# Windowed attention on one core: which tiles of the array make the values of VectorE and ScalarE, and where the two halves of a score pair run

## The chip, the cores and the metric

The kernel runs on one core of one Trainium2 chip. The metric is the device time of one execution in microseconds (us); lower is better. The engines of the core work side by side and wait for one another through semaphores: TensorE (PE in the profile; its weight loads are PEld), VectorE (DVE), ScalarE (ACT), GpSimd (POOL) and SyncE (SP), which here only issues DMAs.

## The reference, cut to what matters

An image of 224 x 224 tokens with 96 channels is projected to q, k and v. The first 48 channels attend within horizontal stripes of 8 rows, the last 48 within vertical stripes of 8 columns. Each stripe has 8 x 224 = 1792 tokens; there are 28 horizontal and 28 vertical ones. The two results are put side by side and projected with `wo`.

```
qkv = einsum('bhwc,cd->bhwd', x, wqkv)
qh, kh, vh = first 48 channels of q, k, v, as 28 stripes of 8 rows   (28, 1792, 48)
oh = softmax(qh @ kh^T * 48**-0.5) @ vh
qv, kv, vv = last 48 channels, as 28 stripes of 8 columns            (28, 1792, 48)
ov = softmax(qv @ kv^T * 48**-0.5) @ vv
out = concat(oh, ov) @ wo
```

## The kernel before, in words

**Stages.** Two stripes are worked on at a time, one in partitions 0 to 63 and one in 64 to 127 (`w` in the code). So there are 28 stages `P`: 0 to 13 for the horizontal stripes, 14 to 27 for the vertical ones. In each stage the 1792 queries are cut into four chunks `c` (512, 512, 512, 256), and the 1792 keys into 28 key tiles of 64.

**Units.** The work on scores comes in units: two key tiles by 512 queries (four key tiles by 256 in the last chunk). A unit's scores (`qk`, L764) fill two PSUM banks, the two *halves* of a pair; each half is written by two matmuls, one per stripe, for each key tile. A unit belongs to ScalarE or to VectorE (L437 to L446):

- A ScalarE unit (`add_a`, L820): scores (stream `a`), one exponential over both banks (`A`, L824) into a tile `PT`, then one value product (`c`).
- A VectorE unit (`add_d`, L832): scores (stream `b`), VectorE turns each half into integers `I_sb` (`j`, L844), and two further tiles `U_sb` and `E_sb` are made from it (L849, stream `U`) by GpSimd, or by VectorE where the order string has a small `u`. Each of the three tiles goes into a value product of its own (`d`, `d`, `D`), so that a VectorE unit has three value products where a ScalarE unit has one.

There are 984 ScalarE units and 388 VectorE units; `ND` = "4442" gives the VectorE units per chunk, so that a stage has 35 ScalarE units and 14 of VectorE (stage 0: 39 and 10).

**Tiles of the array.** With 48 or 49 rows of contraction and 64 or fewer output columns, TensorE is used as four tiles of 64 x 64. A matmul from partitions 64w to PSUM partitions 64w is on a *diagonal* tile (mode `q` in the code), one from 64w to 64 - 64w on an *off-diagonal* tile (mode `v`). The two stripes of one mode go side by side, and the two modes can go side by side too. In general scores are on the diagonal tiles and value products off them; for *turned* key tiles (`turned`, L463: the first 2 x TURN, TURN = 2) it is the other way round. `TD` = "1111" says how many of a chunk's VectorE units are among the turned ones. So before, in each of the first three chunks, units 0 (VectorE) and 1 (ScalarE) are turned, units 2 to 4 are VectorE's and 5 to 13 ScalarE's, not turned.

**Preparation.** While stage P is worked on, `prep` (L506) makes K, Q and V of stage P+1: projections on TensorE, evacuated into `KT_sb`, `QT_sb`, `V_sb` (two buffers each). For it, `blocks` (L403) copies two stripes of x into a DRAM buffer `x_blocks` (two DMAs), and `load` (L413) reads that back transposed (two DMAs) once the copies have landed. In the vertical half, `fin` (L671) writes the stage's output at its end with 24 stores (L760), when the last addition on GpSimd (L733) is done.

**The order of the work** is written out by hand in two strings. In `SEQ` each letter takes the next operation of one stream, so that the order of the letters fixes the order on every engine; `BANK` gives the PSUM bank of each new tile. The letters of SyncE's queue are `x` (start), `X` (block copies and loads) and `y` (stores). Engines take their operations strictly in this order (`emit`, L250): an operation that waits holds up all that is behind it on its engine. Semaphore waits are derived from the operations' dependencies (`place`, L200).

Of the kernel before, what the change touches and what calls it, by code (L numbers as in the profile page):

```python
# [6 lines left out]
BF16 = mybir.dt.bfloat16  # L7
# [9 lines left out]
TURN = 2  # L17
TD = ["1111"]
# [5 lines left out]
def ndc(P, c):  # L24
# [9 lines left out]
    "fDjDAbcaceadfdAjdadaddecUdbAdadjafcDcAXXDebacajcbcUAcajcacbccAjcfaadodffAdbkeUadaddgjADbDacarjcbcAacrackcUjbdA"
    "fcacaejdfdAdabeadfdfUAXjcfabacecdAXcdadjabDdDAjbcacaDjfDAcaceUacDccAbaoaDcjbAgadardUjfdfAdfadradDfeADacaeccbVc"
    "fAajcaccbecAacjacUdbdAajdadbdjbddADaDajDdUDAacDcacbcDcAjdbacacjdUbAcajdadbdAodaDaDdjcdAcUdadagcbcArDcracacDcjA"
    "bcUacajgccAraodardbdgAdajUdadfDrAgarDacecfAcacreacUcbAdardadfdjdAbDaDeaDfDAdjacacdecdUAbdadjaDbDcAXXajcacbccAj"
    "bkcaUcacjcccAfadoadfdfAadaedkdbUcgAjcbDaDajcfcAacraecrbcfUcAjdadadebdAadadjdbdcdAXcjaUbaDdjDDAXabaffjDfAcDeacU"
    "accDAbcacjacccbcAoadaUdfjdAagadedffdfAracracDfDAebaUacecfcAcaedajdbdAadjbdadVdcjdAcbDaDjaDbDAdcUjacacbcdAcjaca"
    "cbcDAcjacUabDoAadadjdgddAdcrabraUcdDjdADbaDajDcbcAacjacfcUcAcaecagccAoadrardggUADaraDrddfrAdbrdacacjbcAUacacef"  # L40
    "cDAjDaDaDbecfAcaceacDdjbkdAadkajdDbdAjaUabdddddAXXjcacacbcAcjbacaUcccjcAfadaodfDfAbDaedadUgdjAdbacacrjcbcAaDra"
    "DDfjUDbAadadejdfdAadeaddcdcAXUbacajbdcdAXcDjabaDcjAcbUacacjcfcfAacaccfcbAoaaUcegAdadrajdfdAdraDaDfefdfAUabaecf"
    "ccjAbcacaecfcAcaVjcacbdedAadjbdadjbdAdUDaDajDdDbAcacjacbcdAcjaUcabdcDjbADcadajdAbdaodaUcdcdjcAdadagcbDrADDraca"
    "UcDcjbAcacajccgcAoaadrdbrUdgAdadrajDfDAdragacecfUAcacreaccfdAraddadbedfAdacajcbDADeaDajbkdDdkAcjdaUdaDbDcAXXaj"
    "cacbccAjbcacaUcjcccAfadoadfdfAadaedbdUDfAjDbcacaejcbcAacajcgdbUdArdajdadfrdAaDeaDdbdDAXUDjdabaccjdcAXfafafcbec"
    "DAacUacjcbcDAcajbacccjcAbadUaodfDAdjadadfdfefAaDageUcbcAracraccfjcAacacebcVcfAjadaddbedAadjbdaUDdDjdADbDacjacb"
    "cAdcjacaUcdbDAcajcabDoAdadadjUgdAdDarDarcdcbAcdajbadcDUcAjgaaccrDcrbAacacjccAUaodadbggAjdadadrdbArDaDarcjfUcAc"
    "acradfdedAadacebcfdAdjacacdDeAUbdaDajDbdADdjaDabcDjAXXcbcUacajcfcAcaecacbccAjafakcUofAdfdaaeddbAgdajdaDbDkrcAr"
    "aUcadjfdbdAcaecjadfcAcaceaUcfdfAXfadeabdDDdAXjafaDdbedADacaUjcDcbAcacjacbcDAcjabacccjcUAbaadodfDffAjadaddfedAa"
    "ceacVDbcfAjcacacbecAacUjadbddjbdAagadjdddDAaDrUaDrDbcdAjcaacbccdAcjabaUcDjcDAbacajdbddAjadacUcbocdAdaadjDgDdAc"  # L50
    "argarcDUcDArcarcacbcAccjcadaodbUAaDjaDcfcdgAbedadacrcjbAUdadadrfddAjgaadeddcAdcUarcarbdcAdDjabaDDjAfDaDaeUfcDc"
    "AXXaceacbccAjbacaccjkcccAfkadoaUdffAdaedadgdbArDfarDaccUejbAcacacjbcfdAdjadadbedAacacjbfdfAXcfjabUacDedDAXdadj"
    "abDdDAjDcacUacbcAcDjacaccccAbaoadUdfdjAdfadaedfDfAaDeagcfUcrAbracacedfAdadaeddjbAcVacajcbccAjbacaccjbDUAddaacj"
    "dcDbADaDjacbcdAcjdUcabaoDADajbadgddAjadUaDdrDdrcAbadajdcbcADcjacUagDcArcbrcacaccjAcaadoUdfdAadeadDgbDArdajcacf"
    "UcrAcbdaedadfdAjdadagebDADaDrajbDAcracUacdjcdAbdadjabcDcAXXDjcacaUcbcAacjacfcccecAfaodadbkdfUAgdjadadfrbDAraDa"
    "ceccAakjacUbddfjdbAdacaecjfdAdaceaUcdDdAXbaDajbdDdDAXDjabaDcUjcbAcacajccffAcfcaeacccUAcboaaddfjDAagaDedffAdfUr"
    "dardacfcAeabacecfdAcaVjcacbceAadjbdaddjbAddacacjUdDDAaDbaDcjbcdAacjacbcdcUAjabacDcjDbAadaodcAcjbUadadgjcdADdad"
    "rabrDdcADcjaUgacDrcAbrcacaccjcAaoadUdbdfAjdadadeDgbADacracjUbccAracagjcfdAdardeadfUdAcracaddecdAbacajDdbdDAjaf"
    "aDeDDDAXXbcaucaccAjbcakcakcjcccAfaodaUdfdfADbaeDaddgjAdbDaDarjUDbDAacracfcjcbAcacaejcfcAbadeaUdDdDAXdjabadddjd"
    "cAXdadabucfAcfacjacfcAbecacacjccAcbaoadUdfcAjaDaDbedfAfadjadfUdbAecaaccfjcAcbeacagcjVAdadadbrdfrdAadaDeUdDjdDA"  # L60
    "bcacjaDcbAcdjacacbUccdAjabaccDjDbAadaodDUAdjbadaDdcjdAcgadarbcrdcADUcacjacbcADcjagaccrcAoaUdardbdgAjdadadbrcfA"
    "rDDajcaUgcAaecacfcrDrAbcacadefdAdajdabdedAdUDaDajDdbAdadjabcDcDAXXjcaUcacbcfAcjacacccecAfaodakdbUDfADfjadadebd"
    "AdgaacrcrckcAUajadfdddbeAacajcbdfdAjcacaDdeDUdAXbdDajbaDDcAXDjabadcjcbUAcacjacffAcfcaeacccAbcUoadadfjdAbadaedf"
    "fAdfjaDgaDecbAUacrjaddbdAracacfcjcAacacVefdcbAecadajdbcdUAcjdcacaDbDAaDjbDacdcjdAbUacajcDbDAaodaddjbgAdaUDarDj"
    "dcdAcdardabcDcAjDgacUacrcbrAacacjccbAcoadajUdbAgdajgaddrdAbrDaDarcjfUcAcacracfcAedadadfedAdUadeabdcdcAjdbaDaDj"
    "dDAafabcecAXXjDDDakcakcbucAacacjbcccccAjafUadodfdfAadaedgdbDArDarcaUcfjcbAcacaejcbdfAdjdadadefUdfAabaDdjDdDAXD"
    "faceabcdAXcDUjabaDcdjcbAacjaccfcAacUeaccccbAoadadfjDfAfabeadgdjAbVdadarDjbcAcacracfUcjAcbcacaeDfDAadeadjdbdUAa"
    "dajddcdcdAcacaDbDDcAjbUcacacjDcAdcabaoddAaDajDUgcDcrDAdrabaddcjbcAdadjaUbcdcAjgaaccrcbrAacacoUcAjadadbDfAjDada"
    "dedgUAbdacracjbccAracagjcfdADarDeaUDfDAdradadDedDAbadajcdUbdcAdjabadcjcAXXfcacaecbcAkcjbackacccjcAUfaadodffAad"
    "eaddgbdArDfarDacUcejbcAacacjbcfDAdjabadedUAadadjbfdfAXfjacacdcedcAXabadjcbcdAaDjaDDfcAuacaccDebDUAcacajbccAoad"  # L70
    "adfjfgAfadeaddfdrAVacracDbeDfAcacaedUdjAabdadjbddddAcjacacbcdDuAaDaDdjDbcAUacjacbccDAjacabcDjbAdaUdajdbdAcajca"
    "cbDAodDadadUjcdgcAacragrDcDcAacracrbcUcAjcccadaodbAdajdadgdfDrADragaUdebdAcacrajdbdAcracacfjcAbadeadUdDdDAjdba"
    "DaDjdcAfaafceDUcDAXXcaceacbcAacjacbccjkcccAafkadodfUdfAadaedgdbDArDarcacfjcbUAcadeajdbdfAdjdadacedcAbcacjabdDd"
    "AXDjabUaDdDjfAXcfafabecDAcDacjUaccbcAajcaccccbAoaaddUfjgAdadaedffdfAracracfDDeAbaUcaecfcAceacajcbdAadjbdadVdjb"
    "AddaDajDdDbDAacuaccdjcbAUcdacjaccbAcDajbacDjAbaUdadoddddAjacacgDDAfrarUaDcDcdAegacacdrcrbAcacajcccAbodajadcbAa"
    "cjbdUaddfjcAadaDeDgbcAcarjgaUcdrAdbadrjaddfdAracacDUdeDdAbaDajbdDdAcDjaDabcUAXXcfjcacaecbcAacjaccccfAkobUdaadj"
    "dffAadeaddbDgAjDackaUcbrcfArcacaecjbdfAccjacacfebfAUaDaDjbfDAXedadadfjdAXdddaeabDdAcdjUacaccbcDAjacaccccbAoaaU"
# [191 lines left out]
def bass_standalone__window_attn_cswin__vision_kernel(  # L269
# [32 lines left out]
    with es:  # L302
# [203 lines left out]
        def prep(P, startup=False):  # L506
# [154 lines left out]
            for f, *args in work:  # L661
                f(*args)
# [272 lines left out]
```

## Time and profile before

| | |
|---|---|
| median of 3 runs | 947.76 us (947.38 to 948.65) |
| the profiled execution's own time | 947.77 us |
| its span, first to last instruction | 945.7 us |
| busy: PE, ACT, DVE, POOL | 99%, 98%, 93%, 81% of the span |
| exponentials on ScalarE (L824) | 984 |
| stores of the vertical half (L760) | 312 in 13 stages |
| block copies (L411), transposing loads (L418) | 54, 54 |
| mean granted TensorE clock | 0.997 |

How to read it: the profile is one execution. Engines' busy shares say which engine could be the limit; matmuls are pipelined, so a busy PE is not PE at its peak. A group of the profile is a line of the code with an engine, an operation and tiles; its numbers are busy time, the mean duration of one, and the idle time of the engine before it with what ended that. Issues of DMAs stand under SPq. The "granted clock" is the share of its full clock that TensorE got.

### The profile page before, as it was taken

Reading aid. Unit: us, or ns where it says so; the run is one execution under the profiler, and the core shown is the slowest. Engines: PE = TensorE matmul, PEld = TensorE weight load, DVE = VectorE, ACT = ScalarE, POOL = GpSimd, SP = SyncE. Lnnn points to the kernel's source line nnn. Section 1 sums busy time; section 2 is a strip of 40 time slices with the busy share of each in tenths; the row PEclk is TensorE's granted clock in tenths of the full one; section 3 lists DMA queues with packets and bytes.
Section 4 is the critical chain, followed back from the end, with each engine's and each line's share of the span. In section 5 each row is a group of like instructions: output and inputs, shape, how many; then the busy total and the mean of one; then the engine's idle time right before and its main releaser. Section 6 shows DMA issues by size and latency. Waiting matters only on the chain.

```text
span 945.7 us, 48281 instructions
## 1 busy us (share of the span) xinstructions
PE 936.0 (99%) x21770; PEld 625.8 (66%) x21770; DVE 881.6 (93%) x1754; ACT 925.2 (98%) x993; POOL 769.2 (81%) x512
## 2 busy tenths in 40 slices
PE   9999999999999999999999999999999999999997
PEld 4666766676776677666666767766666666667664
DVE  8999999999999999999999999999999999999994
ACT  7999999999999999999999999999999999999996
POOL 3778988888886888787898888889879888878883
PEclk9999999999999999999999999999999999999998
DMA  8724513440441343244120515545533534461112
GB/s 141 96 46 72 71 22 53 71 66 9 71 71 22 52 72 47 28 71 71 28 46 10 93 36 81 88 72 86 86 61 67 85 57 81 76 84 30 31 20 44
DMA packets 253254, 57.09 MB, mean 60 GB/s; under 512 B 252936, under 2 KB 252936, under 8 KB 253048
## 3 DMA queue, kind: packets, MB, share of 16 engines
q1 hardware_dynamic: 251464, 53.47, 36.5%
q8 instruction: 170, 2.79, 1.3%
q10 hardware_dynamic: 1584, 0.55, 0.3%
q14 instruction: 36, 0.29, 0.1%
HBM read 19.13 MB, written 28.21 MB: 50 GB/s over the span
## 4 chain that ended last, share of the span: by engine, by line
PE 98%; ACT 1%; DVE 0%; issue 0%
PE ps L804 50%; PE ps L778 36%; PE ps L535 5%; PE ps L637 4%; PE ps L691 1%; PE ps L725 1%; ACT PT L824 1%; PE ps L396 0%; PE ps L602 0%; DVE out_sb L736 0%; PE ps L634 0%; PE ps L496 0%; PE ps L529 0%; DVE OT_sb L870 0%; DVE warm L368 0%
## 5 line engine op out<-in xcount | busy, mean ns | idle before, releaser
L824 ACT ACTIVATE PT<-ps 128x1024 bf16<-128x1024 f32 x984 | 921.2, 1036 | 7.7 <-PE ps L778 3.0
L778 PE MATMUL ps<-QT_sb,KT_sb 49*64 49x512 bf16 (+1 forms) x6272 | 738.8, 354 | 0.7 <-issue 0.6
L844 DVE TENSOR_SCALAR I_sb<-ps 128x512 int16<-128x512 f32 x776 | 511.1, 682 | 21.7 <-PE ps L778 17.2
L804 PE MATMUL ps<-PT,V_sb 64*50 64x512 bf16 (+1 forms) x4496 | 499.4, 350 | 0.2 <-issue 0.2
L778 PEld LDWEIGHTS ps<-QT_sb,KT_sb 49*64 49x64 bf16 x6272 | 282.3, 105 | 159.0 <-ACT PT L824 53.7
L849 POOL TENSOR_SCALAR U_sb<-I_sb 128x2048 int16<-128x2048 int16 x170 | 322.5, 1897 | 55.6 <-DVE I_sb L844 37.0
L849 POOL TENSOR_SCALAR E_sb<-I_sb 128x2048 int16<-128x2048 int16 x164 | 311.1, 1897 | 46.2 <-PE ps L804 18.9
L804 PE MATMUL ps<-U_sb,V_sb 64*50 64x512 bf16 (+1 forms) x1776 | 245.7, 350 | 0.0
L804 PE MATMUL ps<-I_sb,V_sb 64*50 64x512 bf16 (+1 forms) x1776 | 239.7, 352 | 0.2
L804 PEld LDWEIGHTS ps<-PT,V_sb 64*50 64x50 bf16 x4496 | 215.6, 100 | 32.7 <-issue 0.7
L804 PE MATMUL ps<-E_sb,Vs_sb 64*50 64x512 bf16 (+1 forms) x1776 | 233.2, 350 | 0.0
L733 POOL TENSOR_TENSOR out_sb<-tmp,Ph_sb 128x480 bf16<-128x480 f32 (+1 forms) x84 | 85.7, 1028 | 31.0 <-DVE E_sb L849 14.9
L804 PEld LDWEIGHTS ps<-I_sb,V_sb 64*50 64x50 bf16 x1776 | 80.2, 100 | 31.4 <-PE ps L804 8.2
L804 PEld LDWEIGHTS ps<-U_sb,V_sb 64*50 64x50 bf16 x1776 | 89.2, 100 | 14.0
L804 PEld LDWEIGHTS ps<-E_sb,Vs_sb 64*50 64x50 bf16 x1776 | 88.0, 100 | 13.8 <-issue 0.6
L535 PE MATMUL ps<-xa_sb,w_sb 64*64 64x512 bf16 (+3 forms) x440 | 80.2, 356 | 0.2 <-issue 0.2
L870 DVE CAST OT_sb<-ps 128x512 bf16<-128x512 f32 x112 | 68.9, 615 | 9.2 <-PE ps L804 8.5
L535 PE MATMUL ps<-xb_sb,w_sb 64*64 64x512 bf16 (+2 forms) x436 | 77.1, 348 | 0.0
L556 DVE TENSOR_SCALAR_CACHE_REDUCE KT_sb<-ps,bias 128x512 bf16<-128x512 f32 x108 | 72.0, 677 | 1.9 <-PE ps L535 1.5
L549 DVE TENSOR_SCALAR QT_sb<-ps 128x512 bf16<-128x512 f32 (+1 forms) x111 | 67.5, 615 | 3.2 <-PE ps L535 1.8
L637 PE MATMUL ps<-w_sb,xa_sb 64*64 64x48 bf16 x1512 | 65.3, 187 | 0.0
L637 PE MATMUL ps<-w_sb,xb_sb 64*64 64x48 bf16 x1512 | 64.9, 186 | 0.1
(68 smaller groups left out, 604.0 us busy)
## 6 DMA issues: line engine op xcount, KB each, us to landing
x_blocks<-in_x_dram SPq DMA_DIRECT2D x54, 336.0 KB
out_dram<-out_sb SPq DMA_DIRECT2D x104, 42.0 KB
out_dram<-out_sb SPq DMA_DIRECT2D x208, 21.0 KB
out_dram<-out_sb SPq DMA_DIRECT2D x22, 24.0 KB
xa_sb<-x_blocks SPq DMA_TRANSPOSE x27, 5.0
xb_sb<-x_blocks SPq DMA_TRANSPOSE x27, 5.9
Ph_sb<-in_x_dram ACTq DMA_DIRECT2D x1, 336.0 KB, 3.1
out_dram<-out_sb ACTq DMA_DIRECT2D x6, 24.0 KB
```

Of the source, the lines that this page charges most:

```text
L535: ins = e.matmul(out_, lhsT=wt, rhs=rhs, start=i == 0, stop=startup or i == 1)
L549: return e.tensor_scalar(dst, src, QS if startup else A128, None, ALU.mult)
L556: return e.tensor_scalar(dst, src, bias[:, 0:1], None, ALU.add, ALU.add, accum_out=acc)
L637: ins = e.matmul(out_, lhsT=(xa_sb, xb_sb)[i][b][o:o + 64, 0, t0:t0 + 64], rhs=w2_sb[o:o + 64, i, wblk(P, "v"), 0:C2], start=i == 0, stop= ...
L691: ins = e.matmul(bk3[to:to + 64, s, :], lhsT=OT_sb[b][o:o + CA, blk * 64:(blk + 1) * 64], rhs=wo_sb[0][o:o + CA, :], start=True, stop=True)
L733: return e.tensor_tensor(res, tmp[t][:, 0:n, :], ph, ALU.add)
L778: ins = e.matmul(bank(t.k)[to:to + 64, i * qs:(i + 1) * qs], lhsT=KT_sb[b][64 * w:64 * w + CA, 64 * k:64 * k + 64], rhs=QT_sb[b][64 * w:64 ...
L804: ins = e.matmul(bank(k_.slot.k)[to:to + CP, 0:qs], lhsT=V_[o:o + 64, k, :], rhs=rhs()[o:o + 64, h * 512 + i * qs:h * 512 + (i + 1) * qs], ...
L824: a = wk.add("A", Op("act", ACT, lambda e: e.activation(split(PT[i % NPT]), two(ts), ACTF.Exp, scale=LN128), qs_ + pt_free.get(i - NPT, [] ...
L844: ds.append(wk.add("j", Op("dve", 0.6, lambda e, t=t, at=at: e.tensor_scalar(I_sb[y][:, at:at + 512], bank(t.k), one, 0.0, ALU.add, ALU.ma ...
L849: fn = lambda e, dst=dst, c=c: e.tensor_scalar(dst[:, 0:m], I_sb[y][:, 0:m], float(c), 1.0, ALU.add, ALU.mult)
L870: k.evac = wk.add("o", Op("dve", 0.07 + qs / 960, lambda e, k=k, b=P % 2, q0=q0, qs=qs: e.tensor_copy(OT_sb[b][:, q0:q0 + qs], bank(k.slot ...
```

## The change

1. `TURN` goes from 2 to 4 and `TD` from "1111" to "4442": the first 8 of the 28 key tiles are turned, and all VectorE units of a chunk are on them. So VectorE's value products are all on diagonal tiles and its scores off them, and ScalarE's value products are all off the diagonal (but for the first chunk of stage 0, which has no VectorE unit).
2. The two halves of a ScalarE pair's scores are put on different tiles: the first half stays on the diagonal, the second is computed from copies `KS_sb` and `QS_sb` of K and Q in which the two stripes have changed places, off the diagonal. Where the unit's first index is a multiple of 7 (`ALTN`), both halves are off it. This holds for all ScalarE units but those of the very first chunk.
3. The copies are made in each preparation by four DMAs on SyncE, two for K and two for Q, 64 partitions of 3,584 bytes each, in a new stream `w` (`x` in stage 0). A score matmul that reads a copy waits for the last of the four (`alt_ready`).
4. `NY`, the number of buffers of `I_sb` and `U_sb`, goes from 4 to 3. The first part of the value projection is cut in two pieces instead of three. `turn_w` (weights for the mean) moves from stream `f` to `h`, and `blocks(2)` behind the first preparation.
5. `SEQ` and `BANK` are written anew. The counts of the letters are the same but for `f` (493 to 465), `h` (23 to 24), the new `w` (108) and `x` (19 to 23), and `U`/`u`: 334 and 54 before, 321 and 67 after.

What the new `SEQ` gives SyncE's queue in three stages, with the number of exponentials (`A`) that stand in `SEQ` between the stage's first unit and the letter; the next stage's first score matmul stands at 35:

```
stage  9:  w w (K copies) 9 9    X X X X 11 12 19 20                          w w (Q copies) 26 26
stage 19:  w w            7 7    X X 11 11   y x24, 12 to 28   X X 29 30      w w            32 33
stage 25:  w w            7 7    X X 11 11   y x24, 12 to 28                  w w            29 30
```

Stages 1 to 14 are like stage 9; stages 15 to 24 like stage 19 (in stages 16 and 23 the loads too stand behind the stores), with the Q copies' letters 2 to 5 exponentials before the next stage's first score matmul; stages 25 and 26 like stage 25. Before the change the strings gave stage 19: X X 11 11, y x24 11 to 27, X X 28 29.

The diff, without the two strings:

```diff
-TURN = 2
-TD = ["1111"]
+TURN = 4
+ALTN = 7
+TD = ["4442"]
...
-    NPT, NY, NL, NR, NT = 8, 4, 2, 4, 3
+    NPT, NY, NL, NR, NT = 8, 3, 2, 4, 3
...
+        QS_sb = [sb(f"QS_sb{i}", [128, NTOK], BF16) for i in range(2)]
+        KS_sb = [sb(f"KS_sb{i}", [128, NTOK], BF16) for i in range(2)]
...
+        s_alt = [sem(f"s_alt{b}") for b in range(2)]
...
-        blocks(2, "x")
...
-                p, ops = fill("f", 0.2, pe_fn, [op_w0, o_id], [("dve", 0.2, lambda e, bk, a=a: cp(e, bk, *a), [o_wq], True, "e")
+                p, ops = fill("h", 0.2, pe_fn, [op_w0, o_id], [("dve", 0.2, lambda e, bk, a=a: cp(e, bk, *a), [o_wq], True, "e")
...
-                cut = [0, n] if startup else [0, 4, 7, n] if k0 == 0 else [n * i // 3 for i in range(4)]
+                cut = [0, n] if startup else [0, 2 * TURN, n] if k0 == 0 and TURN > 2 else [0, 4, 7, n] if k0 == 0 else [n * i // 3 for i in range(4)]
...
+            war = [o for (_, a, _), o in last_qk.get(prev2, {}).items() if a]
+            for dst, src, ready in ((KS_sb[b], KT_sb[b], k_ready[P]), (QS_sb[b], QT_sb[b], q_ready[(P, NCH - 1)])):
+                for w in range(2):
+                    alt_ready[P] = wk.add("w" if P else "x", Op("sp", 0.64, lambda e, dst=dst, src=src, w=w: e.dma_start(dst[64 - 64 * w:128 - 64 * w, :], src[64 * w:64 * w + 64, :]),
+                                                  [ready] + war, lat=3.0, dma=s_alt[b]))
...
-                def fn(e, t=t, th=th):
+                alt = P + c > 0 and stream == "a" and (h == 1 or kts[0] % ALTN == 0)
+                K_, Q_ = (KS_sb[b], QS_sb[b]) if alt else (KT_sb[b], QT_sb[b])
+
+                def fn(e, t=t, th=th, alt=alt, K_=K_, Q_=Q_):
...
-                            ins = e.matmul(bank(t.k)[to:to + 64, i * qs:(i + 1) * qs], lhsT=KT_sb[b][64 * w:64 * w + CA, 64 * k:64 * k + 64],
-                                           rhs=QT_sb[b][64 * w:64 * w + CA, q0:q0 + qs], start=True, stop=True)
+                            o = 64 - 64 * w if alt else 64 * w
+                            ins = e.matmul(bank(t.k)[to:to + 64, i * qs:(i + 1) * qs], lhsT=K_[o:o + CA, 64 * k:64 * k + 64],
+                                           rhs=Q_[o:o + CA, q0:q0 + qs], start=True, stop=True)
...
+        blocks(2, "x")
```

More of the change, by code (lines that the diff above doesn't have):

```diff
@@ L34 @@
[L34 to L53, printed above, removed]
@@ new lines @@
+    "cdjAaacfcfeAbfUcdeaacdAaaefowddAjfbDwkaDakDeDAbaajXdcfcdcdejAcdUbaafjcbAdaaecXfffAjaaUbdcdecfAcjaacdXgceADcaaU"
+    "DcrfcrfAfXaaebDcDAcdjaabdUcdjAbdaacdjcdbDAaDjaDbDVcAjcaafcocfAcaaeUcdcdAcdebaadwjcdbdAcawjadUbdcDAjcaadcdcDAbD"
+    "bajaDcdUAcdjaagdcdrcdArbaadcdjbdAUcDcDjaacDocAaaDbdcdjgcAUaacdrcdrbdAaacdjbDcDAjDbUaafcjcADaaofcecAgaUradecdAc"
+    "dcraafcAbdeaacdUcdjAdbaadcjfcdAaaebdcgwkjcDAbDkbDwrjaacDAaargUdcdjbdAcdaarjcdfAXrXaadbUfcfDcAeaacDecDjbfAaoaDd"
+    "dcAeaabdcdjbdAcdaajUcffAfjaacfecbdAaaebdcdUcdjAaacgDjcfcfAXfraarcfcUAXeaabDebDcDAcdjaacfcdjAbdVaaecdbdjAwbdaDa"
@@ new lines @@
+    "DjwcDUcDAjaabcocdAbaadjcdcUdAcjaadbdcdAjcaadcdcdAcDubaaDcDjcUADgaadrcdrcdAcaadcdbdAcauaDcDcjDAcDcaoadcdbAdbaja"
+    "dbdcAdjaabdcdjUfcAcjaafccAeaabDcDebDAcDUaajcgcAraodadrcfcAjaagdcdrcdeAUaabdcdrbdAaajbDcDcDjAbaUaDjcgcdAcarajfc"
+    "dcdArdgaaUedcdbrAwbdraacdwjcDAbDaajXcDkbDUcAjaafjAcdafoadXcdcAkdeUaabdcdjfcAdbaadejbfcAcgjUaacdcdrAeaacffrfAbD"
+    "eaacfcjAXcDaabDebDUcdAXaajfcffjAcdaacfecbdUAeaabdcdjcAfadaDebDjcADwbaVaDodwcdAcajadcdUcjdAgdbaradrbdAcDcajadcd"
+    "cUDAjaabDcDjbdAaacdjcdcdAcdUaacdcdAbdaajbDcDAcDjaaUbDcdjcdAbaadjcdcdAaaocdUfccAaaeggcDcDAraarfccUcDrArbaaDcebA"
@@ new lines @@
+    "aoadcjdcAcdaajbdbdAdcjaUafcjcdAcaaedcfcdcAedbaaUgwjbDcADcarwajDbDcdArcaadgjkdbUdAcarajdfdAXrcaXafcdcedAbDkaaUj"
+    "cDfcDADeaodafbcdAceaafffjAbdaaecdUbdAcdjaagcdcjdAbaaDrcjfcUcAaarfcfefbDAXaaecDbDcdjAXVbdaajcdfcAcjaafcUdceAcda"
+    "abdebDjcDAwaDaDjcdwUcdAaaocdcdcdAaabdbdjcdAcUaaDjcdcdAcDbaaDjbDcAaaUjcdbdcAjcdaagdcdArcaradUcdcDAcdbaaDjbDcADc"
+    "ajaUbcAdocaadbjdbdAcaajdcdcUfAjcbaaDecfcAcajagcDAeDUbaaDrogAcrafacrjdcAaacdrbdUcdAeaabdcdjcgAaacdrjfccdUAaargd"
+    "cdebDArcawraDbDcDwjAkbdaakcdjbdAcdjcaUadfjAXdbaafjfcXDAcaaecDUbDcDAejafacocdAbaadebdUcdAcjaaffjfAaacdecdbdAUcd"
@@ new lines @@
+    "jaabdcdjcDAaabDcDjbDAXaaUcdjcdfcAXcaaegccdAaarUbdrcDcDAjfbffjaafcAbeadUadebDAcDaajdcdcocdAaacfVjcddcAaaegdcdwr"
+    "cdArbaUadwcdjbDAcDaajbDcDAjcdaaUbdcdAjcdaabdcdjbdAaacducDcDAcajaDcDcdAobdUbaadjcdAaacgjcdcdcDAraarUfccDAbeaaDc"
+    "DcjfAbaaocecfAaajgcAraaeUdcdccdrAbdaajcdbdAcdjaafcUcdAeDbaaDwjbDcDAcgwjgaadkcdrAcudbaadrcdkcAdUcrajadbdcrDAXXb"
+    "aaDjcDbDAcajadcdcoDAadadcjdfAdcuaaffcdecAdUbaadejbdAfcbjaacDcDAeaagcjcDbdAaarcjfffAXraaUfcecfcAXfefaabdecdAbda"
+    "ajUbdcdAjcDaabDjcDAbDajadVcdcDAjaabDocDfcAcUjaacdcdeAcdaafcgdAeaacdrUwrbdcDAaawjbccjAdbaadjcUdbAdcdjcaadcdAbaa"
@@ L165 @@
+    "53045165304516530431560341562013456514305613451653451673451367154367125431765245176521457652147652145167245067"
+    "12450167045167014506714501674501673450367045306745307653476543672345765243765421374563217567423574562376452376"
+    "54372305437054234754234075423407542340754234075423471540734154034754034754076345036704532670345267325674235674"
+    "235476231457632145327145237451234512745014520145214501452176501247"
 )
@@ L456, in bass_standalone__window_attn_cswin__vision_kernel @@
                 chunks[(P, c)] = k
+        alt_ready = {}
         ksum_op, mean_pe, mean_ev, q_pe, wqT_op = {}, {}, {}, {}, []
@@ L777, in fn @@
                             to = 64 - 64 * w if turn else 64 * w
-                            ins = e.matmul(bank(t.k)[to:to + 64, i * qs:(i + 1) * qs], lhsT=KT_sb[b][64 * w:64 * w + CA, 64 * k:64 * k + 64],
-                                           rhs=QT_sb[b][64 * w:64 * w + CA, q0:q0 + qs], start=True, stop=True)
-                    return ins
-                ops.append(wk.add(stream, Op("pe", S, fn, [k_early[P] if kts[-1] < 2 else k_ready[P], q_ready[(P, c)]], steps=len(kts), take=[t], book=ts[1:] if pair and not h else [], mode="v" if turn else "q")))
-            last_qk[P][stream, turn] = ops[1]
+                            o = 64 - 64 * w if alt else 64 * w
+                            ins = e.matmul(bank(t.k)[to:to + 64, i * qs:(i + 1) * qs], lhsT=K_[o:o + CA, 64 * k:64 * k + 64],
+                                           rhs=Q_[o:o + CA, q0:q0 + qs], start=True, stop=True)
+                    return ins
+                ops.append(wk.add(stream, Op("pe", S, fn, [k_early[P] if kts[-1] < 2 else k_ready[P], q_ready[(P, c)]] + ([alt_ready[P]] if alt else []), steps=len(kts), take=[t],
+                                          book=ts[1:] if pair and not h else [], mode="v" if turn != alt else "q")))
+                last_qk[P][stream, alt, turn] = ops[-1]
             return ops, ts
```

225 lines of the change are left out of this document (111 added, 114 removed).

## The prediction

> **What bounds the kernel now.** I read the page first: busy shares, then the costliest groups. Columns of a group: busy us, mean ns of one, then idle us before them and who ended it.
>
> ```profile
> span 945.7 us, 48281 instructions
> PE 936.0 (99%) x21770; PEld 625.8 (66%) x21770; DVE 881.6 (93%) x1754; ACT 925.2 (98%) x993; POOL 769.2 (81%) x512
> ...
> L824 ACT ACTIVATE PT<-ps 128x1024 bf16<-128x1024 f32 x984 | 921.2, 1036 | 7.7 <-PE ps L778 3.0
> ```
>
> ScalarE is the clock of this kernel: 984 exponentials in one queue, almost no idle. But a busy share hides how far apart they start, so I asked for stretches of line 824 alone (columns: length, ACT busy and count, granted TensorE clock, DMA share, GB/s).
>
> ```profile
> 476.00:872.00 396.00, 393.49 (x420) 1.00 0.42 67
> 905.30:923.50 18.20, 18.20 (x21) 1.00 0.14 27
> ```
>
> Over twelve of the later stages one exponential starts every 396/420 = 0.943 us; in the last stage, where no next stage is prepared, every 18.2/20 = 0.910 us (the 21st is the one in progress at the edge). The reader sees 0.033 us per exponential, 32 us in all, that scores arriving a little late cost ScalarE. That is the most that better-timed scores can win back. A stage of 35 exponentials lasts 33.0 us now.
>
> **The other resource that matters is SyncE's DMA queue.** In the first half it mostly waits for TensorE to be done with the last projections (its row in the waits of SyncE's queue: us in total, times, longest):
>
> ```profile
> SPq L261 <- PE ps L535: 345.2, 15, 28.6
> ```
>
> In stages 15 to 25 it works almost without a pause. Below are its timeline over three such stages and, ahead of it, stretches of line 824 that place them: the count up to 673.6 is 705, so unit 704, the first of stage 20, starts there; 706.8 and 739.8 are one stage later each.
>
> ```profile
> 0.00:673.60 673.60, 658.60 (x705) 1.00 0.39 61
> 673.60:706.80 33.20, 33.00 (x37) 1.00 0.50 77
> 706.80:739.80 33.00, 32.81 (x37) 1.00 0.39 68
> ```
>
> ```profile
> 683.94 15.59 SPq L760 DMA_DIRECT2D out_dram<-out_sb  x24
> 699.58 3.55 SPq L411 DMA_DIRECT2D x_blocks<-in_x_dram  x2
> 710.11 1.36 SPq L418 DMA_TRANSPOSE xa_sb<-x_blocks  x1
> 711.51 2.19 SPq L418 DMA_TRANSPOSE xb_sb<-x_blocks  x1
> 716.99 17.41 SPq L760 DMA_DIRECT2D out_dram<-out_sb  x24
> 734.44 3.71 SPq L411 DMA_DIRECT2D x_blocks<-in_x_dram  x2
> 745.24 1.47 SPq L418 DMA_TRANSPOSE xa_sb<-x_blocks  x1
> 746.75 2.63 SPq L418 DMA_TRANSPOSE xb_sb<-x_blocks  x1
> 750.47 16.48 SPq L760 DMA_DIRECT2D out_dram<-out_sb  x24
> 766.99 4.89 SPq L411 DMA_DIRECT2D x_blocks<-in_x_dram  x2
> 778.10 2.05 SPq L418 DMA_TRANSPOSE xa_sb<-x_blocks  x1
> ```
>
> ```profile
> SPq L418 <- DMA x_blocks<-in_x_dram: 58.8, 9, 7.1
> ```
>
> Each stage: 24 stores, two block copies, a gap, two transposing loads. The last row says what the gap is: the loads wait for the block copies to land (9 times, up to 7.1 us). So the start of the load is the landing: 10.5, 10.8 and 11.1 us after the first copy was issued, mean 10.8. The stores begin 10.3, 10.2 and 10.7 us into their stage, mean 10.4, and take 15.6, 17.4 and 16.5 us, mean 16.5. Today nothing on TensorE needs what SyncE does late in a stage.
>
> **The change, part by part.**
>
> *Counts.* VectorE still has 388 units and ScalarE 984; exponentials and their sizes stay. Nothing there.
>
> *TensorE's two pairs of array tiles.* Per full chunk, in units (one unit's scores or one value product): before, diagonal 12+1+3 = 16 and off-diagonal 2+9+9 = 20; after, diagonal 4.5+12 = 16.5 and off-diagonal 4+10+5.5 = 19.5. Over a stage the fuller side falls by about one unit in 70. Nearly nothing by itself.
>
> *The pair side by side.* Now the second half of ScalarE's scores runs on the other tiles beside the first, so the pair is ready a pass earlier. A pass is 0.217 us (starts of following pairs in this stretch):
>
> ```profile
> 445.34 0.38 PE L804 MATMUL ps<-I_sb,V_sb 64*50 64x512 bf16 x2
> 445.55 0.38 PE L804 MATMUL ps<-PT,V_sb 64*50 64x512 bf16 x2
> 445.77 0.38 PE L804 MATMUL ps<-PT,V_sb 64*50 64x512 bf16 x2
> ```
>
> It can win at most the 0.033 us per exponential, 1.15 us a stage; at least nothing, since TensorE's total hardly changes. I take 0.5 us a stage, near the middle.
>
> *One buffer fewer for I and U; 13 more U or E on VectorE* (67 instead of 54 in the order string).
>
> ```profile
> L849 DVE TENSOR_SCALAR E_sb<-I_sb 128x2048 int16<-128x2048 int16 x30 | 21.0, 700 | 0.1
> L849 POOL TENSOR_SCALAR U_sb<-I_sb 128x2048 int16<-128x2048 int16 x170 | 322.5, 1897 | 55.6 <-DVE I_sb L844 37.0
> ```
>
> VectorE gains 13 x 0.70 = 9.1 us and stands at 891; GpSimd loses 13 x 1.90 = 24.7. Covered by VectorE's 64 idle us; were that cover gone, 9 us. The value projection in two pieces, `turn_w` in another stream and `blocks(2)` after the first preparation: no work added, nothing.
>
> *The swapped copies.* Per stage four DMAs on SyncE, 64 rows of 3,584 bytes each; 112 in all. As issues they cost 4 x 0.65 = 2.6 us of SyncE (15.59/24 per store), hidden in its gaps. But they add a wait: the second half of the very first ScalarE pair of each stage needs all four. TensorE works in order, so behind that matmul stand all scores and value products of the stage, and ScalarE has one or two finished pairs left to work on. So the question is when the last copy of Q lands.
>
> In stages 0 to 14 the order string puts these two DMAs 7 or more exponentials (6.6 us) before they are needed and SyncE has nothing else to do: no cost. At the end of stages 15 to 24 it puts them *behind* the 24 stores and the two block copies, 2 to 5 exponentials before the need. In stages 25 and 26 there are no block copies: the last copy is issued at 10.4 + 16.5 + 1.3 = 28.2 us, early enough.
>
> For the ten stages, worked out from the rows above: stores begin 10.4, end 26.9; block copies land 10.8 later, 37.7; if the queue keeps its order, the Q copies (448 KB) follow them. Three rows on rate and order, from the timeline, from the DMA view of 618 to 623 us, and from the page:
>
> ```profile
> 619.62 16.96 SPq L760 DMA_DIRECT2D out_dram<-out_sb  x24
> ```
>
> ```profile
> GB/s 0 8 8 10 8 10 10 186 293 293 293 263 291 295 285 283 293 293 293 291 289 291 283 293 199 94 61 57 89 92 54 0 0 15 89 63 5 0 146 94
> ```
>
> ```profile
> Ph_sb<-in_x_dram ACTq DMA_DIRECT2D x1, 336.0 KB, 3.1
> ```
>
> The second is the rate in 40 slices of 618 to 623 us. Stores were issued from 619.62 on, yet the transposes' 293 GB/s run on to 621.0 and only then the stores' own rate appears: what was issued first goes first. At 293 GB/s, 448 KB take 1.6 us: landed at 39.3. Scores (two passes, 0.4) and the hand-over to ScalarE after it, 0.6 (an estimate): the stage takes 39.9 us instead of 33.0. The other end, no order in the queue: the last issue is at 26.9 + 4.1 (block issues: 3.55, 3.71, 4.89) + 0.65, and lands 3.1 us later (third row) at 34.8; with 0.6, 35.4. I take the first, because the only row that shows two transfers close together shows them in order.
>
> The Trainium skill, "DMA: Bandwidth & Descriptors", section "Queues, rings and completion order", says the same with more force: each engine consumes descriptors in ring order and the semaphore increment lands only after every earlier write from that engine. By it the stage is 39.9, without it 35.4.
>
> *The clock behind the stall.* TensorE then stands idle for some 6 us per stage, which it never does now. The end of this trace is the only place that shows what idling does:
>
> ```profile
> 939.00:940.00 1.00, 0.17 (x8) 0.03 (x5) 0.73 (x4) 0.00 (x0) 0.00 (x0) 1.00 0.26 50
> 941.00:942.00 1.00, 0.00 (x0) 0.00 (x0) 0.00 (x0) 0.00 (x0) 0.00 (x0) 0.50 0.40 76
> ```
>
> ```profile
> L778 PE MATMUL ps<-QT_sb,KT_sb 49*64 49x512 bf16 (+1 forms) x6272 | 738.8, 354 | 0.7 <-issue 0.6
> L396 PE MATMUL ps<-warm 128*128 128x512 bf16 x9 | 4.0, 631 | 1.2 <-DVE warm L368 1.2
> ```
>
> In the stretches (PE's busy time first, the clock third from the end) the granted clock is 0.50 within 2 us of the last matmuls. How long it needs to come back no row shows; the nine warm-up matmuls at the start ran 4.0 us at 631 ns each (score matmuls later: 354). Cost per stage: nothing, or 4.0 us at half speed, 2.0. I take 0.9, as TensorE has some slack and the stores wait for only a third of the stage. The stage: 40.8.
>
> The skill's "TensorE: Matmul & The Clock Gate", section "Why this matters for your kernels", warns of gaps over about 3 us and needs some 3.4 us of activity to return to full clock. An estimate from that page: 1.7 us lost per stall, the stage 41.6.
>
> **The sum.** Ten stages x (40.8 - 33.0) = +78. Eighteen other stages x -0.5 = -9. On the profiled execution's 947.8 us (span 945.7 and 2.1 around it; the median of the three runs is 947.76, the same): 947.8 + 78 - 9 = 1017.
>
> **Rivals.**
> - *The copies are in time and ScalarE gets its scores sooner.* It needs SyncE to reach the Q copies some 6 us earlier than rows say. For it: the 0.033 us. Half of it on all 28 stages gives 947.8 - 16 = 932. Against: the timeline above.
> - *Late but not queued behind the block copies*: 10 x (35.4 - 33.0) - 9 = +15, 963.
> - *The clock takes the full 2.0*: 10 x (41.9 - 33.0) - 9 = +80, 1028; upper edge with stores at 17.4 us each time, 1037.
> - *It does nothing*: the copies are just in time and the pair's order moves nothing, 948.
>
> **How the numbers follow.** Forecast 1017: 0.50; full clock loss 0.18; late without queue 0.10; win 0.19; nothing 0.03. The forecast's own range is 990 to 1037. To leave out no more than 0.2, the range keeps the late case and nothing: 945 to 1038. About 0.2% is what a measurement of this kernel tells from no change. Faster 0.19, same 0.03, slower 0.78.
>
> **What would show it.** Right: in the changed profile TensorE's and ScalarE's digits drop at ten places in the second half, one per stage; score matmuls wait for the DMAs into QS_sb, 4 to 7 us each; the first half is a little quicker per exponential; the clock falls beside the gaps. Wrong: the second half runs at 33 us a stage, or the waits stand in the first half too, or VectorE, now at 891 us, becomes what ScalarE waits for.

## The result, and the profile after

| | before | after |
|---|---|---|
| median, us | 948.2 (947.38 to 949.17, 4 runs) | 1303.11 (1302.23 to 1303.24, 4 runs) |
| ratio, 95% interval | | 1.373 (1.371 to 1.375) |
| span of the profiled execution, us | 945.7 | 1300.4 |

The change costs 355 us. I had predicted 1017, 69 us of loss, with 1038 as the upper edge: the sign was right, but by luck: the size was not, and the wait that was to bring the loss, for late copies, is hardly there. The page of the changed kernel: busy shares, the chain of waits by engine and by line, and the costliest groups.

```profile
span 1300.4 us, 48695 instructions
...
PE 1054.3 (81%) x21770; PEld 579.4 (45%) x21770; DVE 923.7 (71%) x1767; ACT 971.8 (75%) x993; POOL 745.0 (57%) x499
...
PEclk9999999999999999999999999999999999999999
...
ACT 45%; PE 44%; issue 5%; DVE 3%; SPq 2%; DMA 0%; ACTq 0%; POOL 0%; DVEq 0%
...
L839 ACT ACTIVATE PT<-ps 128x1024 bf16<-128x1024 f32 x984 | 967.8, 1027 | 316.7 <-PE ps L792 186.5
...
L792 PE MATMUL ps<-QS_sb,KS_sb 49*64 49x512 bf16 (+1 forms) x2386 | 409.1, 364 | 236.0 <-ACT PT L839 227.8
L792 PE MATMUL ps<-QT_sb,KT_sb 49*64 49x512 bf16 (+1 forms) x3886 | 525.8, 352 | 1.3 <-DVE KT_sb L574 0.7
```

No engine is full any more. An exponential still takes 1.03 us, but ScalarE is idle for 317 us before them (8 us before the change), waiting for scores. The scores that come late are those from the *copies*: TensorE is idle for 236 us before them, and what ended 228 us of that is line 839, an exponential; before scores from the originals it is idle for 1.3. So TensorE waits for ScalarE and ScalarE for TensorE. The chain of waits shows the same. Its line by engine stands in the fence above (ACT 45%, PE 44%); this is the one of before:

```profile
PE 98%; ACT 1%; DVE 0%; issue 0%
```

Before, the chain ran along TensorE alone. After, it changes hands between the two engines nearly half and half: a loop. Stretches of line 839 (length, ACT busy and count, clock, DMA share, GB/s) give its speed: from the first unit of stage 1 to that of stage 14, and from stage 15 to stage 25, where I had expected the stalls:

```profile
56.30:686.20 629.90, 453.41 (x456) 1.00 0.30 54
...
735.90:1174.40 438.50, 340.95 (x350) 1.00 0.42 76
```

One exponential starts every 629.9/455 = 1.38 us in the first half (the 456th is the one in progress at the edge) and every 438.5/350 = 1.25 us in the second, where it was 0.943. So there are no ten dips: the whole run is slow, the first half more than the second, and the clock stays at full speed.

The loop itself, in the changed kernel's timeline (start, duration, engine, line, operation; in brackets the idle time before and who ended it):

```profile
143.75 1.02 ACT L839 ACTIVATE PT<-ps 128x1024 bf16<-128x1024 f32 x1 [0.56 <-PE ps L819]
...
144.82 0.40 PE L792 MATMUL ps<-QS_sb,KS_sb 49*64 49x512 bf16 x2 [0.53 <-ACT PT L839]
...
145.33 1.02 ACT L839 ACTIVATE PT<-ps 128x1024 bf16<-128x1024 f32 x1 [0.56 <-PE ps L792]
...
146.40 0.40 PE L792 MATMUL ps<-QS_sb,KS_sb 49*64 49x512 bf16 x2 [0.52 <-ACT PT L839]
```

The exponential ends at 144.77; 0.05 later a score matmul that waited for it starts; 0.51 after that start comes the next exponential. The period is 1.02 + 0.05 + 0.51 = 1.58 us. Why does a score matmul wait for the exponential that is running? Because it writes into a bank that this exponential is reading. `BANK` says so: in this stretch the pairs are (3,4), (5,4), (3,4), (5,4): bank 4 is in every one. In the old string pairs alternate between (6,7) and (4,5). Counted over the strings, the bank of the second half was last held by the exponential *just before* in 527 of 984 pairs after, in none before, when 920 came from the exponential two before. I call such a pair shared. 527 x (1.58 - 0.943) = 336, close to the 355 lost. The two stretches bear it out: 305 of the 455 pairs of stages 1 to 13 are shared and 152 of the 350 of stages 15 to 24, which by the same sum gives 1.37 and 1.22 us per exponential, where 1.38 and 1.25 were measured.

The waits on the copies, where I had put the loss (us in total, times, longest):

```profile
PEld ps L792 <- ACT PT L839: 458.8, 629, 1.4
...
PE ps L792 <- ACT PT L839: 228.1, 496, 1.0
...
PEld ps L792 <- DMA QS_sb<-QT_sb: 0.4, 1, 0.4
```

One wait of 0.4 us for a copy, hundreds for ScalarE.

### The profile page after: what moved, and what is told of

Same layout as the page of the kernel before. It is cut to its first block, busy times and chain, and to the rows that moved or that the text cites. A ratio compares the mean times of both kernels' runs of the same rounds, so it can differ in the third digit from the quotient of the medians.

```text
span 1300.4 us, 48695 instructions
## 1 busy us (share of the span) xinstructions
PE 1054.3 (81%) x21770; PEld 579.4 (45%) x21770; DVE 923.7 (71%) x1767; ACT 971.8 (75%) x993; POOL 745.0 (57%) x499
## 4 chain that ended last, share of the span: by engine, by line
ACT 45%; PE 44%; issue 5%; DVE 3%; SPq 2%; DMA 0%; ACTq 0%; POOL 0%; DVEq 0%
ACT PT L839 45%; PE ps L792 25%; PE ps L819 15%; DVE I_sb L859 2%; PE ps L642 1%; SPq L770 1%; PE ps L540 1%; PE ps L735 1%; SPq L671 0%; DVE KT_sb L561 0%; PE ps L701 0%; DMA QS_sb<-QT_sb 0%; ACTq L263 0%; PE ps L401 0%; SPq L416 0%
## 5 line engine op out<-in xcount | busy, mean ns | idle before, releaser
L839 ACT ACTIVATE PT<-ps 128x1024 bf16<-128x1024 f32 x984 | 967.8, 1027 | 316.7 <-PE ps L792 186.5
L819 PE MATMUL ps<-PT,V_sb 64*50 64x512 bf16 (+1 forms) x4496 | 603.9, 350 | 1.0 <-ACT PT L839 0.6
L792 PE MATMUL ps<-QS_sb,KS_sb 49*64 49x512 bf16 (+1 forms) x2386 | 409.1, 364 | 236.0 <-ACT PT L839 227.8
L792 PE MATMUL ps<-QT_sb,KT_sb 49*64 49x512 bf16 (+1 forms) x3886 | 525.8, 352 | 1.3 <-DVE KT_sb L574 0.7
L864 POOL TENSOR_SCALAR U_sb<-I_sb 128x2048 int16<-128x2048 int16 x161 | 305.4, 1897 | 293.6 <-DVE I_sb L859 269.5
L792 PEld LDWEIGHTS ps<-QS_sb,KS_sb 49*64 49x64 bf16 x2386 | 119.7, 104 | 472.7 <-ACT PT L839 431.2
L819 PE MATMUL ps<-U_sb,V_sb 64*50 64x512 bf16 (+1 forms) x1776 | 263.7, 352 | 0.0
L819 PE MATMUL ps<-I_sb,V_sb 64*50 64x512 bf16 (+1 forms) x1776 | 256.7, 353 | 0.0
L792 PEld LDWEIGHTS ps<-QT_sb,KT_sb 49*64 49x64 bf16 x3886 | 186.5, 106 | 108.4 <-ACT PT L839 27.6
L819 PEld LDWEIGHTS ps<-I_sb,V_sb 64*50 64x50 bf16 x1776 | 82.0, 100 | 10.6 <-DVE I_sb L859 2.1
L647 DVE CAST V_sb<-ps 128x480 bf16<-128x480 f32 (+1 forms) x84 | 52.2, 622 | 46.0 <-PE ps L642 23.2
```

The costliest lines, as they stand in the source:

```text
L647: return e.tensor_copy(V_sb[b][:, k0:k0 + n, 0:C2], bk[:, 0:n * C2].rearrange("p (j c) -> p j c", j=n))
L792: ins = e.matmul(bank(t.k)[to:to + 64, i * qs:(i + 1) * qs], lhsT=K_[o:o + CA, 64 * k:64 * k + 64], rhs=Q_[o:o + CA, q0:q0 + qs], start=Tr ...
L819: ins = e.matmul(bank(k_.slot.k)[to:to + CP, 0:qs], lhsT=V_[o:o + 64, k, :], rhs=rhs()[o:o + 64, h * 512 + i * qs:h * 512 + (i + 1) * qs], ...
L839: a = wk.add("A", Op("act", ACT, lambda e: e.activation(split(PT[i % NPT]), two(ts), ACTF.Exp, scale=LN128), qs_ + pt_free.get(i - NPT, [] ...
L864: fn = lambda e, dst=dst, c=c: e.tensor_scalar(dst[:, 0:m], I_sb[y][:, 0:m], float(c), 1.0, ALU.add, ALU.mult)
```

## The experiments

**1. The old kernel with shared banks, and the changed kernel without.** Theory: shared banks make the loss. Rivals: the second halves on the other tiles, the copies.

```diff
 BANK = (            # old_kernel_shared_banks: the old kernel, this string alone
-    "76543210765432076123546702314670123067123067123167023106712301670231675023516702356710235671235167523167512356"
+    "76543210765432076123542360147216034623601621434023601432140164236120453265013462304516340125014523412034502351"
...
 BANK = (            # banks_apart: the changed kernel, this string alone
-    "76543210765432017543271024571045204521045061204562104562014562106540121640325126632051263205106235016235601523"
+    "76543210765432017543210752102745771245712745671254671254671256745214567514327654723475642374567234567234756423"
...
```

> The kernel before, nothing changed but the bank string: 526 of its 984 pairs now write their second half into the bank of the exponential just before, as many as in the changed kernel. Bank theory: 948 + 526 x 0.66 = 1295, 1200 to 1330. Tile and copy theories: 948 to 980, since no tile and no DMA is changed.

> The changed kernel with its order of work untouched, only the PSUM banks given out anew, so that 6 score pairs instead of 527 write their second half into the bank that the exponential just before is still reading. Bank theory: each of the 521 gives back about 0.66 us (an exponential every 1.58 us in the locked stretches against 0.92): 1303 - 344 = about 960, up to 1020 if the late copies of Q then show at the ends of stages 15 to 24. Tile theory (scores on the off-diagonal tiles are slow beside the value products there): stays above 1250. Copy theory (the DMAs of the swapped copies hold the pairs up): stays above 1250 too, since the DMAs are not touched.

Measured: 1255.54 us (one execution) for the old kernel with 526 shared pairs (947.59 before), and 1136.24 for the changed kernel with 6 (ratio 1.199, 1.196 to 1.201). Dealing banks alone costs the old kernel 308 us, 0.59 per shared pair (not all of it need be the pairs': with this string 288 of VectorE's 776 halves of scores also take a bank that an exponential held last, 90 before), and its page shows the changed kernel's loop:

```profile
ACT 52%; PE 40%; issue 6%; DVE 1%; DMA 0%; ACTq 0%; POOL 0%; POOLq 0%
...
L824 ACT ACTIVATE PT<-ps 128x1024 bf16<-128x1024 f32 x984 | 968.5, 1022 | 270.0 <-PE ps L778 207.4
```

That shared banks suffice for a loss of this size is shown. In the changed kernel they were worth 167 us, 0.32 per pair; the other 189 were still there, so this run missed what I expected of it. In banks_apart the chain is back on TensorE (68%), with a new partner at 20%, VectorE, and these waits:

```profile
PE 68%; DVE 20%; ACT 5%; issue 3%; DMA 3%; POOL 1%; SPq 0%; ACTq 0%; POOLq 0%; DVEq 0%
...
PEld ps L792 <- DVE I_sb L859: 97.1, 219, 1.4
ACT PT L839 <- PE ps L792: 92.5, 172, 4.6
...
PEld ps L792 <- ACT PT L839: 62.6, 168, 1.3
...
PEld ps L792 <- DMA QS_sb<-QT_sb: 14.4, 8, 3.3
```

Scores now wait for banks that VectorE is reading (line 859).

**2. Both halves on the same tiles; the old order with the halves split.**

```diff
-                alt = P + c > 0 and stream == "a" and (h == 1 or kts[0] % ALTN == 0)
+                alt = False                      # one_tile_pair: the changed kernel
```

> The changed kernel with both halves of every ScalarE pair on the diagonal again, from the unswapped K and Q; order, banks and the copies' DMAs stay, but nothing waits for the copies. Bank theory: the shared banks stay, so 1280 to 1400. Tile theory: back to 950 to 1000. Copy theory: back to 950 to 1000.

> The kernel before, its order, banks and VectorE units kept, with only the second halves of ScalarE's pairs put on the off-diagonal tiles and the swapped copies made (their DMAs right behind the last evacuation of K and of Q). To make room it has 6 PT tiles instead of 8, a bfloat16 tmp (rounded more coarsely) and no warm tile of its own. Bank theory: its pairs reuse banks of two exponentials before, so it stays near 948, 935 to 975. Tile theory: above 1200. Copy theory: above 1100.

Measured: 1334.84 us (one execution), and 1125.04 (ratio 1.188, 1.185 to 1.191). Taking the halves together again wins nothing, which speaks against the split as what costs the 355 us. It is no clean test of the split alone: per full chunk the diagonal tiles then carry 10 units of scores and 12 value products of VectorE, 22 x 0.433 = 9.5 us (two passes of 0.217 each), more than ten exponentials at 0.910.

old_order_pairs missed what I expected, and by my own mistake. Splitting the halves in the old order moves 4.5 units per chunk from the diagonal to tiles that already had 20: 24.5 x 0.433 = 10.6 us a chunk, where ten exponentials take 9.1. Its page:

```profile
PE 1097.2 (97%) x21770; PEld 723.4 (64%) x21770; DVE 913.2 (81%) x1754; ACT 984.9 (87%) x993; POOL 770.4 (68%) x512
...
PE 95%; DMA 3%; DVE 1%; ACT 1%; SPq 0%; issue 0%; ACTq 0%
```

TensorE bounds it (95% of the chain), and by the count above one pair of its tiles does, so it says nothing on the split either. To price the rest of that kernel (copies, six PT buffers instead of eight), I ran it with the halves put back:

> The kernel before, its order, banks and tiles untouched, with the four copies of K and Q per stage issued right behind the last K and the last Q evacuation, and nothing that waits for them (both halves of a pair stay on the same tiles); to make room, six PT buffers instead of eight, tmp in bf16, and the warm-up tile laid into out_sb. It is old_order_pairs (1125 us) without the second halves moved. If that run lost by the load on the off-diagonal tiles: 945 to 955 us here, so the copies as traffic and the smaller buffers cost nothing. Rival (the copies or the buffers took a good part of the 177 us): 980 us or more. It also prices the prediction's step that the copies cost nothing as issues.

Measured: 952.08 us (ratio 1.003, 1.0015 to 1.005). The 112 DMAs of the copies and the smaller buffers cost 1 to 5 us when nothing waits for them. In old_order_pairs something does: the 3% of its chain on DMA, some 30 of its 177 us, are waits for the Q copies, and no run takes these away.

**3. Is dealing anew harmless, and what is one bank worth?** Two more strings for the old kernel, nothing else changed: all eight banks with no pair shared, and seven banks.

> The kernel before with nothing changed but its bank string, dealt anew by the same rule that gave the changed kernel its apart banks: a pair's banks come from the exponential two before or earlier in all 984 pairs. Control for the runs in which banks were dealt anew. Bank theory (only who held the bank before counts): no change, 945 to 960 us; it has 44 first halves that take a bank freshly read by VectorE's line 844, up to 0.3 us each, so at most +13. Rival (a string dealt by this rule costs by itself, and that is what the changed kernel with apart banks still loses): 1000 us or more.

> The kernel before, its order and its tiles untouched, dealt onto seven PSUM banks instead of eight (after the warm-up the eighth is not used). Of the 984 second halves 791 then come from the exponential two before, and some 180 take a bank that VectorE has just read; in the changed kernel with apart banks the same counts are 790 and some 180. Theory (the changed kernel with apart banks still lives with too few banks, since it holds 2.1 accumulators where the old one holds 1.5): the loss comes back here though nothing else of the change is in it, 1100 us or more, and PE's weight loads of scores wait for line 844. Rival (what it still loses comes from the order of the work, one buffer fewer for I and U, or the copies): under 1000 us.

Measured: 959.58 us (ratio 1.012, 1.011 to 1.014) and 1267.43 (1.337, 1.334 to 1.340). The control is at the top of its range: dealing anew costs 12 us, not 190. One bank less costs 320 us, though only six second halves are shared. The seven-bank kernel's waits have the face of banks_apart, only more of it:

```profile
PEld ps L778 <- DVE I_sb L844: 221.7, 408, 1.2
ACT PT L824 <- PE ps L778: 198.5, 410, 1.3
DVE I_sb L844 <- PE ps L778: 184.8, 387, 1.6
```

So the old order, as it is written, needs all eight banks. In the changed order accumulators stay longer: counted over the strings, one is held, from its first value product to its evacuation, for 18.4 exponentials instead of 13.0 (2.1 accumulators alive on average instead of 1.5). The code says why: turned value products have to come ahead of a chunk's others (`o.sync = k_.early`), and now all twelve of VectorE's are turned, so a chunk opens its accumulator while the one before is still in use. That scarce banks cost this much is shown; that the longer tenancy is what makes them scarce is argued from the counts.

**4. The copies, once the banks are out of the way.**

```diff
-    "fcfAfeUaaybcedAcyaajdcfcycAjaagcUydecfcAdcyraaedbrdycAdbaajdycqDcDAbjayadbdjcVDybAaajDcydbdcAjadyadUbdjbdAyaaj"
+    "fcfAfeUaaybcedAcyaajdcfcycAjaagcUydecfcAdcyraaewwdbrdycAdbaajdycqDcDAbjayadbdjcVDybAaajDcydbdcAjadyadUbdjbdAya"
...
```

(In each of stages 15 to 24 the two `w` of the Q copies stand right behind the `e` that evacuates the last of Q, among the `y`, and are gone from behind the `X`.)

> The changed kernel with its banks apart (1136 us), and in stages 15 to 24 the Q copies issued right behind the last Q evacuation, in the midst of the 24 stores, instead of behind the stores and the block copies. Prediction's theory (these stages end with a wait for the Q copies): the gaps before the first exponential of stages 16 to 25, 2 to 5.6 us, go; the chain of that kernel has 2.6% of 1135 us, 30 us, on the copies: 1100 to 1112 us. Rival (TensorE is short of banks there anyway and what is won at the start of a stage is lost again behind it): 1125 to 1140 us.

Measured: 1121.48 us (ratio 1.183, 1.181 to 1.185), 15 less than banks_apart and between the two ranges: no wait for a copy is left in its trace, but only half of the 30 us that the chain had on them came back. The stall that I had predicted is real in banks_apart. In its timelines of SyncE and ScalarE the two block copies and the Q copies stand behind the stores, and the first exponential of the next stage comes after 4.56 us of idling:

```profile
919.94 5.98 SPq L770 DMA_DIRECT2D out_dram<-out_sb  x9
925.96 4.30 SPq L416 DMA_DIRECT2D x_blocks<-in_x_dram  x2
930.31 4.64 SPq L671 DMA_DIRECT2D QS_sb<-QT_sb  x2
```

```profile
928.66 6.03 ACT L839 ACTIVATE PT<-ps 128x1024 bf16<-128x1024 f32 x6 [0.15 <-PE ps L792]
939.25 2.02 ACT L839 ACTIVATE PT<-ps 128x1024 bf16<-128x1024 f32 x2 [4.56 <-PE ps L792]
```

**5. The same change, ordered anew; and the old kernel too.** If the loss lies in the two strings, other strings must win it back with the code untouched.

> The changed kernel's code as it is (tiles, halves side by side, copies, three buffers), with its order string and its bank string written anew: letters were moved, one or a few at a time, wherever that shortens the waits on banks and buffers with the durations that the traces show; the letters are the same but for 33 u instead of 67. Of the 984 second halves 26 take a bank from the exponential just before (527 in the changed kernel); an accumulator is held for 16.6 exponentials (18.4 there, 13.0 before); Q copies are issued as soon as Q is evacuated, 8 us ahead of their use in stages 14 and later. Theory A (the loss lies in the order and the banks as written, not in what is placed where): 950 to 985 us. Theory B (with all of VectorE's value products on one pair of tiles, and ahead of ScalarE's in each chunk, two accumulators overlap whatever the order, and eight banks are too few): 1060 us or more, with weight loads that wait for VectorE's line 859.

> The kernel before with its order and bank strings written anew in the same way and with the same effort, code untouched. It says what the change's placement costs or wins when both are ordered alike. ScalarE's 984 exponentials at 0.910 us, the start and the end set a floor of some 920 us. If the old order is already as good as this way of ordering gets: 940 to 950. If the 0.033 us per exponential that scores come late can be won by order alone: 925 to 940, and the change's placement, at 950 or more, has then nothing that the old one lacks.

Measured: 992.91 us (ratio 1.047, 1.046 to 1.048) and 965.42 (1.018, 1.017 to 1.019; above both ranges that I had given). The code of the change, with all its value products, halves, copies and three buffers where the change puts them, loses 45 us instead of 355. Its page:

```profile
PE 88%; DVE 5%; POOL 3%; ACT 1%; issue 1%; DMA 1%; ACTq 0%; POOLq 0%; DVEq 0%
...
L839 ACT ACTIVATE PT<-ps 128x1024 bf16<-128x1024 f32 x984 | 928.3, 1031 | 46.8 <-PE ps L792 25.1
```

That is 8 us above the range of theory A and far below theory B. The loss lies mostly in the strings; which part of the last 143 us (1136 - 993) is order, banks, the earlier Q copies or the 33 `u` instead of 67 is not told apart. That overlapping accumulators rule out a better order falls: an accumulator is held for 16.6 exponentials here, and the pairs are still apart. My ordering is no better than the old one, though: it makes the old kernel 17 us slower. Ordered alike, the change stands 27.5 us behind the old placement. Waits do not explain it: those of score weight loads on VectorE's integers are alike (change ordered anew, then old kernel ordered anew), and those on exponentials differ by 28 us, but the kernel before, at 948 us, has as many of these (last row).

```profile
PEld ps L792 <- ACT PT L839: 52.2, 204, 0.6
PEld ps L792 <- DVE I_sb L859: 40.9, 148, 1.4
```

```profile
PEld ps L778 <- DVE I_sb L844: 37.9, 135, 1.6
...
PEld ps L778 <- ACT PT L824: 23.7, 108, 0.4
```

```profile
PEld ps L778 <- ACT PT L824: 53.7, 218, 0.5
```

The busy shares (same order) show where the 27.5 us are:

```profile
PE 973.0 (98%) x21770; PEld 615.8 (62%) x21770; DVE 900.0 (91%) x1733; ACT 932.3 (94%) x993; POOL 811.3 (82%) x533
```

```profile
PE 943.7 (98%) x21770; PEld 641.0 (67%) x21770; DVE 889.5 (92%) x1733; ACT 928.0 (96%) x993; POOL 812.7 (84%) x533
```

TensorE is idle for as long in both (18.9 and 20.0 us of the spans of 991.9 and 963.7), but busy for 29.3 us longer with the change, with as many matmuls that last as long each. So by the profile, in which the ends of matmuls are modelled, fewer of them run side by side; why, no run shows.

Whether still better strings would make the placement win is open too.

## Why the prediction was wrong, point by point

- **The failed step** is the part on the pair side by side: "at least nothing, since TensorE's total hardly changes". Together with "*Counts.* ... Nothing there" it took it that new strings serve the same work as well as the old ones. I had both bank strings before me and did not ask, pair by pair, who held the bank last. The price of that is what the runs show: 527 shared pairs, 167 us by banks alone, 310 by new strings as a whole (1303 - 993). What the rest of the 310 is made of is not shown; the longer-held accumulators are a cause argued from counts.
- **What bounds the kernel.** I read ScalarE's 98% as the clock. The chain of waits of before, which I did not use, has TensorE on 98% (value products 50%, scores 36%): TensorE was on the chain almost all the time, and scores came just in time. That is the reading that warns of a change to when scores may start.
- **The swapped copies.** The sum's one large term, +78 for late copies, did not come. Its mechanism was right, the condition was not there. I had the Q copies land 39.3 us into a stage of 33.0. After, a stage of that stretch lasts 43.9 us (438.5/10), so they are in time, and the wait is 0.4 us in all. With the banks apart a stage of the same stretch lasts 402.4/10 = 40.2 us (fence below), the copies are late by a little (longest wait 3.3), and taking the lateness away wins 15 us instead of the 78 of the sum.

```profile
617.00:1019.40 402.40, 336.48 (x350) 0.99 0.47 83
```

- **Other 18 stages 0.5 us quicker each.** Not seen; in the first half a stage lasts 629.9/13 = 48.5 us. The prize was also read too large: in the page's row ScalarE is idle for 7.7 us before all its exponentials, so that the 32 us are not waiting that the profile shows. The gain of the split by itself is not measured: every kernel with it differs in more, or is short of one pair of tiles.
- **One buffer fewer, 13 more U or E on VectorE.** As predicted in size: 67 of them, 23.4 + 22.9 us against 38.1 before, +8.2 for +9.1; VectorE, 71% busy, has room for them. What the missing buffer costs by itself no run shows; the change ordered anew has it too, and loses 45 us in all.

```profile
L864 DVE TENSOR_SCALAR E_sb<-I_sb 128x2048 int16<-128x2048 int16 x34 | 23.4, 689 | 0.0
L864 DVE TENSOR_SCALAR U_sb<-I_sb 128x2048 int16<-128x2048 int16 x33 | 22.9, 693 | 0.3
```

- **The clock.** No loss in the changed kernel: TensorE is idle often, but for 0.5 us at a time, and the granted clock is 0.998 on average. In banks_apart it shows once, at the longest of the eight waits for a copy, and there it is larger than my bound of 2.0 us; see below.
- **The rivals.** None had the banks in it. A rival of the form "a wait that takes the place of the one removed" was asked for by the change itself, which writes a pair's halves in a new order into newly dealt banks; the prediction has it on SyncE only.

## What to carry to other kernels

When a change brings a new order or new buffer numbers, follow each buffer that is used again: who held it last, how long ago, and is that one still reading. A pair that takes over a bank from the step just before turns two engines that overlapped into two that take turns (up to 0.59 us per pair in the old kernel, 0.64 by the period of the loop; taking the sharing away gave back 0.32 in the changed kernel, where other waits took its place), and neither counts of work nor busy shares of before show it. If the chain of waits of before lies on one engine at 98%, look first for new waits on that engine.

## What the hardware showed that I had not expected

The clock behind a stall, in stretches of banks_apart (PE busy first, granted clock third from the end):

```profile
936.00:937.00 1.00, 0.00 (x0) 0.00 (x0) 0.01 (x1) 0.00 (x0) 1.00 (x1) 1.00 0.89 249
...
938.00:939.00 1.00, 0.49 (x6) 0.35 (x10) 0.00 (x0) 0.00 (x0) 1.00 (x1) 0.50 0.00 0
939.00:940.00 1.00, 1.00 (x18) 0.81 (x14) 0.29 (x1) 0.76 (x1) 0.26 (x1) 0.50 0.00 0
```

```profile
943.00:944.00 1.00, 1.00 (x14) 0.50 (x10) 0.45 (x1) 0.76 (x2) 0.00 (x0) 0.50 0.00 0
944.00:945.00 1.00, 0.90 (x10) 0.34 (x10) 1.00 (x5) 0.66 (x1) 0.00 (x0) 0.69 0.00 0
945.00:946.00 1.00, 1.00 (x24) 0.66 (x22) 0.79 (x3) 0.37 (x1) 0.47 (x1) 1.00 0.00 0
```

TensorE has no matmul from 935.5 to 938.5. The clock is halved before the gap ends, and comes back only some 6 us after work has resumed (938.5 to about 944.6, from the 0.69 of that microsecond): an estimated 3 us of TensorE's time lost to one gap. A gap of 2.6 us in the same trace, up to 898.5, leaves the clock at full speed. The Trainium skill, "TensorE: Matmul & The Clock Gate", section "What's actually happening", has some 3.4 us both for the fall and for the return; here the clock fell within a gap of 3.0 us, and the return took some 6, longer than the page has it. On the banks the Trainium skill has the rule that shared pairs break: "Perfetto Trace Analysis", section "Optimizing Tensor Performance", wants independent groups of matmuls to rotate through PSUM banks so that the evacuation of one overlaps the matmuls of the next. The trace of the changed kernel agrees: where the bank is shared, the score matmul starts only 0.05 us after the exponential has ended. The old kernel with shared banks puts up to 308 us on it.
